# Two early blocks of the first expert in unsplit fp32 inside the last routing step, and every split of its weights behind the branch

## The chip, the cores and the metric

The kernel is one program on one core of a Trainium2 chip. The metric is its device time in microseconds (us), the median of the runs. TensorE (PE) multiplies; its weight loads are shown apart as PEld. VectorE (DVE), ScalarE (ACT) and GpSimd (POOL) work on elements, and SyncE (SP) issues most of the transfers. Each engine works through its own instructions in order and waits for the others by semaphores.

## The reference, cut to what matters

```python
def _moe_ref(x, w_gate, w_local, w1, w2):
    logits = np.einsum('bsd,de->bse', x, w_gate)
    local_gate = 1.0 / (1.0 + np.exp(-np.einsum('bsd,de->bse', x, w_local).squeeze(-1)))
    for b in range(B):
        prev_e = -1
        for s in range(S):
            fresh_e = int(np.argmax(logits[b, s]))
            e = fresh_e if s == 0 or local_gate[b, s] < 0.5 else prev_e
            prev_e = e
            ...
            h = np.maximum(x[b, s] @ w1[e], 0.0)
            out[b, s] = p[e] * (h @ w2[e])      # p: softmax of the logits
```

Ahead of it stands attention over the 32 largest scores (4 batches, 8 heads, 576 tokens, heads of 64). Its output, 4 x 576 tokens of 512 numbers, goes through this mixture of 8 experts with a hidden width of 1024, and the result through a Fourier mixing and a feed-forward layer. Everything is fp32.

## The kernel before

**Stages.** Attention runs first, in 16 pairs of heads with 9 tiles each; a batch is routed as soon as its last tile is done. The routing of the last batch, the *tail*, runs when attention has nothing left. Then all engines load the flag `slow_i` and branch (L1029, L1030; the branch to the exact path isn't taken). Behind the branch come the experts, in the order of their load (rank 0 to 7), then the mixing and the last layer.

**Split products.** The experts' products are made of three products of halves (`fp32r`): a high part (`whi`, `xh`, `hh`) times a high part, high times low, low times high. A weight unit of 128x2048 comes by one SP transfer of 1 MB into `raw` (two buffers), ACT writes `whi` (L214), and DVE or POOL writes `wlo = raw - whi` (L215), each in two halves of 1024 columns. A rank has four units, `wunits[0..3]` for rank 0: first and second layer of hidden blocks 0 to 3, then of blocks 4 to 7. For block f, `mm1` (L1151) makes 12 products, ACT `hh` (relu, L1155), DVE `hl` (L1156), and two steps later `mm2` (L1175) adds 6 products to the sum.

**Early rows.** Rank 0's expert is known after the third batch. Its first 256 rows (`EARLY`, in `xe`) are there before the tail; the other 256 rows come with the last scatter. Blocks f = 0 to 2 (`EF = 3`) of the early rows are done by `early_layers` inside the tail (L591, L604): a generator whose pieces `spend(us)` hands to PE between the routing's own products. Before that, `early_x` transposes the early rows on PE (L572) and splits them (L574 on ACT, L575 on DVE); units 0 and 1 are split between the last tiles of attention, halves of unit 2 on POOL in the tail, unit 3 behind the branch.

**The tail's chain.** DVE turns the last sums `st_x` into logits (`ri` L627, `ltt` L630, L657) and one-hot rows `dl` (L683). PE turns `dl` over (L692), DVE scans it to `er` and `po` (L700 to L708), PE turns those back (L715), DVE makes `oh` and the scatter's indices (L723 to L736), POOL scatters the tokens in five transfers (L751), and DVE and PE rank the experts and write `slow_i` (L776).

**Behind the branch.** SP loads the late rows; PE turns the four chunks of 128 rows (L1105), ACT and DVE split them (L1107, L1108). A hand-written plan then lists the blocks, (rank, f, early rows or not), `mm2` two steps behind `mm1`; splits, loads and a conversion of other weights (`fr`, `fa`, L1126 and L1050) are placed at certain steps of it. The products' results have two buffers, so a block's `mm1` waits until relu and `hl` of the block two before it are done.

```python
plan = [(0, f, True) for f in range(EF, 8)] + [(r, f, False) for r in range(E) for f in range(8)]
```

Of the kernel before, what the change touches and what calls it, by code (L numbers as in the profile page):

```python
# [104 lines left out]
def body(ctx: ExitStack, tc, q, k, v, w_gate, w_local, w1, w2, ch1, ch2, ts, tcd, tnd, tid, out, dbg=None):  # L105
# [76 lines left out]
    slot = [consts.tile([8, 1], F32, name=f"slot{b}") for b in range(B + 1)]  # L182
    DVE.tensor_scalar(slot[0], pcol[0:8], float(XC), None, op0=OP.mult)

    EARLY, EF = 256, 3
    late0 = consts.tile([8, 1], F32, name="late0")
    DVE.tensor_scalar(late0, pcol[0:8], float(XC), float(EARLY), op0=OP.mult, op1=OP.add)
    pv0 = consts.tile([128, 2, 1], F32, name="pv0")
    sid0 = consts.tile([128, 2, 1], I32, name="sid0")
    em0 = consts.tile([128, 2, 1], F32, name="em0")  # L190

    W = {}
    n_u = [0]

    def unit(key, src, dims, pool=None):


        if pool is None:
            pool = (wring, wring, wring, wring, wring2, wring2)[n_u[0] % 6]
            n_u[0] += 1  # L200
        raw, hl = [], []

        def load():
            raw.append(raws.tile([128, 2048], F32, name="raw", tag="raw"))
            SP.dma_start(raw[0].rearrange("p (c f) -> p c f", c=dims), src)

        def split(j, eng):
            if not hl:
                p = pool[0] if isinstance(pool, list) else pool
                hl.extend(p.tile([128, 2048], F32R, name=nm, tag="w") for nm in ("whi", "wlo"))  # L210
                W[key] = tuple(t.rearrange("p (c f) -> p c f", c=dims) for t in hl)
            hi, lo = hl
            cs = slice(1024 * j, 1024 * (j + 1))
            ACT.activation(hi[:, cs], raw[0][:, cs], AF.Copy)  # L214
            eng.tensor_tensor(lo[:, cs], raw[0][:, cs], hi[:, cs].bitcast(F32), op=OP.subtract)  # L215

        return load, split
# [53 lines left out]
    def attention(exact):  # L271
# [3 lines left out]
        with ExitStack() as ph:  # L275
# [10 lines left out]
            spb = acc[:, :, 0:288]  # L286
            if exact:
                for c in range(2):
                    PE.matmul(acc[:, c], W[0, 0, 1][0][:, 0, 0:128], W[0, 0, 1][0][:, 0, :], start=False, stop=True)
            rank_ps[0] = tkp  # L290
            ub = ps.tile([128, 512], F32, name="u", bufs=1)
            up = ub[:, 0:2 * VW].rearrange("p (s d) -> p s d", s=2)
# [271 lines left out]
            def early_x(c):  # L564

                if c == 0:
                    XE["hl"] = [ap.tile([128, 2, S], F32, name="kt", bufs=4).rearrange("p s c -> p (s c)")[:, 0:4 * EARLY]
                                .rearrange("p (d n) -> p d n", d=4) for _ in range(2)]
                x, (xh, xl) = xe, XE["hl"]
                p = next_wide()[:, 0:512]  # L570
                for d in range(4):
                    PE.transpose(p[:, 128 * d:128 * d + 128], x[:, c, 128 * d:128 * d + 128], ident)  # L572
                pr, n = p.rearrange("p (d n) -> p d n", d=4), slice(128 * c, 128 * c + 128)
                ACT.activation(xh[:, :, n].bitcast(F32R), pr, AF.Copy)  # L574
                DVE.tensor_tensor(xl[:, :, n].bitcast(F32R), pr, xh[:, :, n], op=OP.subtract)  # L575
                if c == 1:
                    DVE.tensor_copy(pv0, x[:, :, DM:DM + 1])
                    rows_of(sid0, x[:, :, DM + 2 * IW:DM + 2 * IW + 1], em0)

            def early_layers():  # L580

                xh, xl = (t.bitcast(F32R) for t in XE["hl"])
                hb = [[t.rearrange("p s c -> p (s c)")[:, EARLY * k:EARLY * k + EARLY] for k in range(3)] for t in qpb]
                pb = (wide[0][:, 0:EARLY], wide[1][:, 0:EARLY], wide[1][:, 512:512 + EARLY])
                for j in range(EF + 2):
                    if j < EF:
                        wh, wl = W[0, 0, 0]
                        p, fs = pb[j % 3], slice(j * 128, (j + 1) * 128)
                        for n, (a, x) in enumerate(((wh, xh), (wh, xl), (wl, xh))):
                            for d in range(4):  # L590
                                PE.matmul(p, a[:, d, fs], x[:, d], start=(n == 0 and d == 0), stop=(n == 2 and d == 3))  # L591
                            yield
                        hh, hl = hb[0][j % 3], hb[1][j % 3]
                        ACT.activation(hh.bitcast(F32R), p, AF.Relu)
                        DVE.scalar_tensor_tensor(hl.bitcast(F32R), p, 0.0, hh, op0=OP.max, op1=OP.subtract)
                    if j in (1, 2) and not exact:
                        wunits[2][1](j - 1, POOL)
                    if j >= 2:
                        f = j - 2
                        hh, hl = (t[f % 3].bitcast(F32R) for t in hb)  # L600
                        wh, wl = W[0, 0, 1]
                        for n, (a, w) in enumerate(((hh, wh), (hh, wl), (hl, wh))):
                            for c in range(2):
                                PE.matmul(acc[:, c], a[:, c * 128:c * 128 + 128], w[:, f, :],  # L604
                                          start=(f == 0 and n == 0), stop=False)
                            yield

            early = []

            def spend(us):  # L610
                while early and us > 0:
                    if next(early[0], 1):
                        early.pop()
                    us -= 0.47

            TK = {}

# [33 lines left out]
            def tokens(b):  # L651
# [57 lines left out]
                yield  # L709
                for o, r in ((8, er), (0, po)):  # L710
                    if b == B - 1:
                        spend(1.4 if o else 0.9)
                    for t in range(5):
                        m = 128 if t < 4 else LAST
                        PE.transpose(pt[0:m, t, o:o + 8], r[:, 128 * t:128 * t + m], ident[0:8, 0:8])  # L715
# [46 lines left out]
                    early_load(ex)  # L762
                if b == B - 1:
                    yield
                    if not exact:
                        check_end(chk.pop())
                    for _ in ranks(cnt[B], spend):
                        yield
                    spend(0.5)

                    ov = ap.tile([8, 1], F32, name="ov", bufs=1)
                    DVE.tensor_tensor(ov, cnt[B], capv, op=OP.is_gt)
                    p = tkp
                    PE.matmul(p[0:1, 0:1], ov, ones8[:, 0:1], start=True, stop=True)
                    yield
                    DVE.tensor_scalar(slow_i, p[0:1, 0:1], fail_f, 0.0, op0=OP.add, op1=OP.is_gt)  # L776
# [26 lines left out]
                chk.append(km)  # L803

            def check_end(km):
                p = tkp
                PE.transpose(p[0:1, 0:128], km[:, 0:1], ident)
                kr = ap.tile([1, 1], F32, name="kr", bufs=1)
                DVE.tensor_reduce(kr, p[0:1, 0:128], axis=AX.X, op=OP.min)
                DVE.tensor_scalar(fail_f, kr, 0.5, None, op0=OP.is_lt)  # L810
                DVE.tensor_copy(fail_i, fail_f)
# [86 lines left out]
            for n in range(n_tile + 1 + max(OFF.values())):  # L898
# [22 lines left out]
                    use_consts()  # L921
                if n == n_tile - 1 + OFF["z"]:
                    tok.append(check())
                e = n - n_tile - 3
                if e in (3, 4):
                    early_x(e - 3)
                if 2 <= e < 6:
                    wunits[(e - 2) // 2][1](e % 2, DVE)
                    if e % 2:
                        wunits[2 + (e - 2) // 2][0]()  # L930
            early.append(early_layers())
            for g in tok:
                for _ in g:
                    pass
# [131 lines left out]
    with ExitStack() as ph:  # L1066
# [135 lines left out]

        load_slots(0)
        p0 = prep(0)
        for o in p0[:2]:
            o()
        pops, us, spl = p0[2:], [], []
        for h in range(2):
            wunits[3][1](h, DVE)
        LAG = 2  # L1210
        plan = [(0, f, True) for f in range(EF, 8)] + [(r, f, False) for r in range(E) for f in range(8)]
        for j in range(len(plan) + LAG):
            if j < len(plan):
                r, f, early = plan[j]
# [1 line left out]
            if j >= LAG:  # L1216
                r2, f2, early2 = plan[j - LAG]
                mm2(r2, f2, early2)
                if f2 == 7 and not early2:
                    finish(r2)  # L1220
            if j < 8 - EF:
                if j in (3, 4):
                    pops.pop(0)()
                continue
            if j == 8 - EF:
                exs += [nc.values_load(exi[0:1, x:x + 1], engines=[mybir.EngineType.SP], min_val=0, max_val=E - 1)
                        for x in range(1, E)]
                load_slots(1)
                f64_load(0)
                f64_load(1)  # L1230
            if j == 10 - EF:
                POOL.dma_start(tst, ts)
            if j == 18 - EF:
                POOL.dma_start(tct, tcd)
                POOL.dma_start(tnt, tnd)
            if f in (0, 3, 4, 7) and spl:
                for h in range(2):
                    spl[0](h, DVE)
                spl.pop(0)
            if j >= len(plan):  # L1240
                continue

            if f in (0, 4):
                us = expert_units(r + 1, exs[r + 1], f // 4) if r + 1 < E else mix_units(f // 4)
                if r + 1 == E and f == 4:
                    m1 = list(us)
            if f in (0, 1, 4, 5):
                load, split = us.pop(0)
                if r + 1 < E or f < 2:
                    load()  # L1250
# [364 lines left out]
```

## Time and profile before

| what | us |
|---|---|
| runs | 1263.56, 1265.39, 1265.83 (median 1265.39) |
| the profiled execution | 1266.99 |
| its span, first to last instruction | 1264.8 |
| PE busy | 1194.6 (94% of the span) |
| DVE, ACT, POOL busy | 866.9, 676.3, 446.0 |

The span is 2.2 us shorter than its own execution's time. PE is busy nearly everywhere, except around the tail and the branch, which lie between about 473 and 511 us. A row of the timeline gives start, length, engine, line, operation, output and inputs, and in brackets how long the engine had been idle and what ended that.

### The profile page before, as it was taken

The numbers are of one execution on the slowest core, as the hardware profiler recorded it, in microseconds if no ns is written. First come the engines' busy times: TensorE is split into PE (matmuls) and PEld (weight loads), VectorE is DVE, ScalarE is ACT, GpSimd is POOL, SyncE is SP. The second block draws the span as 40 slices with busy tenths as digits, with TensorE's granted clock in tenths as the row PEclk, the third lists the DMA queues.
The fourth block names the chain that finished last, engine by engine and source line by source line (L and its number), as shares of the span: only waits on it lengthen the run. The fifth ranks groups of instructions, "written<-read, shape, count | busy, mean of one in ns | idle before, by whom it ended". The sixth has DMA issues, their size and how long they took to land. (4 is left out here: it accounts for less than half of the span.)

```text
span 1264.8 us, 25173 instructions
## 1 busy us (share of the span) xinstructions
PE 1194.6 (94%) x8691; PEld 1086.4 (86%) x8691; DVE 866.9 (69%) x3559; ACT 676.3 (53%) x1426; POOL 446.0 (35%) x553
## 2 busy tenths in 40 slices
PE   6999999999998995999999995979999999999997
PEld 5999889998998994898888885869999999999996
DVE  7999999999998985475666665847744444443222
ACT  6999999999997992354444542323322222221110
POOL 3767776786875683011111102713200000000122
PEclk9999999999998998999999995989999999999998
DMA  5757634443451413876666756632310010100111
GB/s 113 193 149 199 143 86 116 115 103 86 124 131 44 138 49 109 259 270 216 213 228 218 231 174 191 194 115 80 102 67 34 34 67 20 49 1 1 50 51 51
DMA packets 125653, 152.25 MB, mean 120 GB/s; under 512 B 68175, under 2 KB 70471, under 8 KB 125402
## 3 DMA queue, kind: packets, MB, share of 16 engines
q1 hardware_dynamic: 120442, 133.34, 36.8%
q0 software_dynamic: 5072, 17.19, 3.8%
q8 instruction: 71, 1.16, 0.4%
q14 instruction: 68, 0.56, 0.1%
HBM read 92.05 MB, written 32.79 MB: 99 GB/s over the span
## 5 line engine op out<-in xcount | busy, mean ns | idle before, releaser
L474 POOL TENSOR_TENSOR y<-ss,g 128x576 f32<-128x576 f32 x144 | 185.3, 1287 | 116.2 <-ACT g L469 58.3
L448 DVE MAX8 cd<-ss 128x8 f32<-128x72 f32 x1152 | 218.2, 220 | 10.0 <-ACT ss L442 9.5
L1529 ACT ACTIVATE fhh<-f 128x256 fp32r<-128x256 f32 x144 | 55.1, 383 | 278.9 <-PE f L1525 274.4
L1530 DVE SCALAR_TENSOR_TENSOR fhl<-f,fhh 128x256 fp32r<-128x256 f32 x144 | 60.9, 423 | 205.9 <-ACT fhh L1529 205.8
L545 PE MATMUL u<-in_v,et 128*128 128x74 f32 (+1 forms) x1600 | 185.5, 265 | 4.9 <-DVE dv L704 2.5
L545 PEld LDWEIGHTS u<-in_v,et 128*128 128x128 f32 (+1 forms) x1600 | 177.5, 181 | 10.0 <-ACT st_x L552 4.0
L528 PE MATMUL tp<-ident,z 128*128 128x128 f32 x720 | 142.6, 284 | 4.8 <-DVE lo L355 4.6
L529 PE MATMUL tp<-huge_id,bb 128*128 128x128 bf16 x720 | 131.7, 220 | 0.3 <-ACT bb L507 0.3
L435 PE MATMUL acc<-kt,qp 128*128 128x288 f32 x640 | 125.2, 323 | 6.3 <-ACT ss L442 4.0
L1550 POOL DMA_INDIRECT out_dram<-ut,orow x18 | 17.5, 971 | 319.4 <-DVE ut L1546 317.5
L469 ACT ACTIVATE g<-ss,mt 128x576 bf16<-128x576 f32 x144 | 118.0, 819 | 5.4 <-DVE mt L462 5.2
L528 PEld LDWEIGHTS tp<-ident,z 128*128 128x128 f32 x720 | 106.4, 148 | 15.6 <-POOL z L516 3.4
L507 ACT ACTIVATE bb<-ss,kth 128x576 bf16<-128x576 f32 x144 | 117.1, 813 | 0.0
L479 DVE MAX8 y<-y 128x8 f32<-128x576 f32 x144 | 107.0, 743 | 5.6 <-POOL y L474 5.6
L516 POOL TENSOR_SCALAR z<-ss,mt 128x576 f32<-128x576 f32 x144 | 107.8, 749 | 5.2 <-PE tp L529 5.2
L534 ACT ACTIVATE et<-tp 128x640 f32<-128x640 f32 x144 | 106.6, 740 | 2.4 <-PE tp L529 1.9
L442 ACT ACTIVATE ss<-acc 128x576 f32<-128x576 f32 x144 | 99.8, 693 | 11.6 <-PE acc L435 8.5
L941 POOL DMA_INDIRECT xm_d<-ysb,sid x23 | 24.6, 1068 | 228.8 <-ACT ysb L1187 225.1
L435 PEld LDWEIGHTS acc<-kt,qp 128*128 128x128 f32 x640 | 94.1, 197 | 9.7 <-ACT ss L442 5.0
L1525 PEld LDWEIGHTS f<-nxh,whi 128*128 128x128 f32 x576 | 87.8, 188 | 14.2 <-issue 1.2
L215 DVE TENSOR_TENSOR wlo<-raw,whi 128x1024 fp32r<-128x1024 f32 x70 | 85.5, 1260 | 14.8 <-ACT whi L214 14.4
L1541 PE MATMUL f<-whi,fhh 128*128 128x512 f32 x288 | 91.6, 399 | 0.7 <-ACT fhh L1529 0.7
(283 smaller groups left out, 2778.9 us busy)
## 6 DMA issues: line engine op xcount, KB each, us to landing
raw<-in_moe_w_dram SPq DMA_DIRECT2D x32, 1024.0 KB
kt<-hi SPq DMA_DIRECT2D x60, 144.0 KB
kt<-lo SPq DMA_DIRECT2D x60, 144.0 KB
xs_d<-xtok SPq DMA_DIRECT2D x8, 1056.0 KB
fr<-in_moe_w_ch_dram SPq DMA_DIRECT2D x16, 512.0 KB
raw<-in_moe_w_ch_dram SPq DMA_DIRECT2D x16, 512.0 KB
md<-md_d SPq DMA_DIRECT2D x9, 516.0 KB
in_k<-in_k_dram SPq DMA_DIRECT2D x32, 128.0 KB
```

The lines of the kernel that those rows point to most:

```text
L435: PE.matmul(p, QP[i][:, s, o:o + 128].bitcast(F32R), KT[i][j][:, s, c].bitcast(F32R), start=(s == heads[0] and j == 0), stop=(s == heads[- ...
L442: ACT.activation(t.rearrange("p (h c) -> p h c", h=2), spb, AF.Copy)
L448: return [lambda j=j: DVE.max(cd[:, 8 * j:8 * j + 8], SS[n][:, 72 * j:72 * j + 72]) for j in range(8)]
L469: ACT.activation(g, SS[n], AF.Sign, bias=MT[i][:, t, 1, 7:8], scale=-SCL, accum_out=DIF[n])
L474: POOL.tensor_tensor(y, SS[n], LT[n], op=OP.mult)
L479: DVE.max(y8, Y8[n])
L507: ACT.activation(t, SS[n], AF.Relu, bias=kth[:, n:n + 1], scale=-1.0)
L516: POOL.tensor_scalar(ZZ[n], SS[n], -1.0, MT[i][:, t, 0, 0:1], op0=OP.mult, op1=OP.add)
L528: PE.matmul(o, z[:, k], ident, start=True, stop=False, is_transpose=True)
L529: PE.matmul(o, bb[:, k], huge_id, start=False, stop=True)
L534: ACT.activation(et, TP.pop(n).rearrange("p (c n) -> p c n", c=5), AF.Exp, scale=-1.0)
L545: PE.matmul(p[0:m, s, 0:VW], et[:, kc, qs], vv[:, kc, VC[s]], start=(kc == 0), stop=(kc == 4))
```

## The change

`EF` falls from 3 to 2. `early_layers` now multiplies the unsplit `raw` weights by an unsplit copy of the early rows, in plain fp32: 8 products of 256 columns (L585), 4 of 512 (L592), and a relu on ACT for each block; a piece is one product, and `spend` counts 0.47 for the smaller and 0.93 for the larger. `early_x` makes one copy on ACT only, one step sooner. No unit is split and none of units 2 and 3 is loaded before the branch. Behind it, ACT and DVE split units 0 and 1 between the first two chunks of rows, SP loads units 2 and 3, and these are split at steps 1 and 2 of a new plan. The end of the check (`check_end`) goes behind two steps of the ranking. (Lines of the kernel after are 12 to 15 smaller than those of before.)

```diff
-    EARLY, EF = 256, 3
+    EARLY, EF = 256, 2
...
                 for d in range(4):
-                    PE.transpose(p[:, 128 * d:128 * d + 128], x[:, c, 128 * d:128 * d + 128], ident)
-                pr, n = p.rearrange("p (d n) -> p d n", d=4), slice(128 * c, 128 * c + 128)
-                ACT.activation(xh[:, :, n].bitcast(F32R), pr, AF.Copy)
-                DVE.tensor_tensor(xl[:, :, n].bitcast(F32R), pr, xh[:, :, n], op=OP.subtract)
...
+                    PE.transpose(p[:, 128 * d:128 * d + 128], xe[:, c, 128 * d:128 * d + 128], ident)
+                ACT.activation(XE["t"][:, :, 128 * c:128 * c + 128], p.rearrange("p (d n) -> p d n", d=4), AF.Copy)
...
-                    if j in (1, 2) and not exact:
-                        wunits[2][1](j - 1, POOL)
...
+                for f in range(EF):
+                    p = wide[1][:, 512 * f:512 * f + EARLY]
+                    for d in range(4):
+                        PE.matmul(p, w1_[:, d, 128 * f:128 * f + 128], XE["t"][:, d], start=(d == 0), stop=(d == 3))
+                        if d < 3:
+                            yield 0.47
+                    ACT.activation(hb[f], p, AF.Relu)
+                    yield 0.47
+                for f in range(EF):
+                    for c in range(2):
+                        PE.matmul(acc[:, c], hb[f][:, 128 * c:128 * c + 128], w2_[:, f, :], start=(f == 0), stop=False)
+                        yield 0.93
...
-                if 2 <= e < 6:
-                    wunits[(e - 2) // 2][1](e % 2, DVE)
-                    if e % 2:
-                        wunits[2 + (e - 2) // 2][0]()
+                e = n - n_tile - 1
+                if e in (4, 5):
+                    early_x(e - 4)
             early.append(early_layers())
+            spend(1.8)
...
         p0 = prep(0)
-        for o in p0[:2]:
-            o()
-        pops, us, spl = p0[2:], [], []
+        p0[0]()
         for h in range(2):
-            wunits[3][1](h, DVE)
+            wunits[0][1](h, DVE)
+        p0[1]()
+        for h in range(2):
+            wunits[1][1](h, DVE)
+        for load, _ in wunits[2:]:
+            load()
+        for f in range(EF, 4):
+            mm1(0, f, True)
+        for f in range(EF, 4):
+            mm2(0, f, True)
+            p0[f]()
+        pops, us, spl = [], [], []
         LAG = 2
-        plan = [(0, f, True) for f in range(EF, 8)] + [(r, f, False) for r in range(E) for f in range(8)]
+        plan = [(0, f, False) for f in range(4)] + [(0, f, e) for f in range(4, 8) for e in (True, False)]
+        plan += [(r, f, False) for r in range(1, E) for f in range(8)]
...
+            if j in (1, 2):
+                for h in range(2):
+                    wunits[j + 1][1](h, DVE)
```

DVE in the tail before, from the end of the check's work to the reduction that begins the routing's chain (`kt` are the split early rows):

```order
L215 TENSOR_TENSOR wlo<-raw,whi 128x1024
L627 TENSOR_SCALAR ri<-st_x 128x5 x2
L628 RECIPROCAL ri<-ri 128x5x2
L630 TENSOR_TENSOR ltt<-st_x,ri 128x5x9 x2
L575 TENSOR_TENSOR kt<-tp_148,kt 128x4x128
L577 COPY pv_128<-xe 128x2
L257 TENSOR_SCALAR em_130<-xe 128x2
L258 SCALAR_TENSOR_TENSOR sid_129<-xe,em_130 128x2
L215 TENSOR_TENSOR wlo<-raw,whi 128x1024 x2
L657 TENSOR_REDUCE dv<-ltt 128x45
```

The same piece after:

```order
L570 COPY pv_128<-xe 128x2
L258 TENSOR_SCALAR em_130<-xe 128x2
L259 SCALAR_TENSOR_TENSOR sid_129<-xe,em_130 128x2
L615 TENSOR_SCALAR ri<-st_x 128x5 x2
L616 RECIPROCAL ri<-ri 128x5x2
L618 TENSOR_TENSOR ltt<-st_x,ri 128x5x9 x2
L645 TENSOR_REDUCE dv<-ltt 128x45
```

The splits and the subtraction of the early rows are gone from between `ltt` and its reduction, and the three small operations stand ahead of `ri`.

PE in the tail before, from the products of `dl` to those of `po`:

```order
L692 MATMUL u<-ident,dl 8x64
L591 MATMUL tp_149<-kt,whi 128x256 x8
L591 MATMUL tp_149<-kt,wlo 128x256 x4
L715 MATMUL u<-ident,er 128x8 x4
L715 MATMUL u<-ident,er 64x8
L591 MATMUL tp_149<-kt,whi 128x256 x8
L715 MATMUL u<-ident,po 128x8 x4
```

The same piece after, with the early products ahead of `dl`:

```order
L585 MATMUL tp_149<-kt,raw 128x256 x7
L680 MATMUL tp_148<-ident,dl 8x128 x3
L680 MATMUL u<-ident,dl 8x128
L680 MATMUL u<-ident,dl 8x64
L585 MATMUL tp_149<-kt,raw 128x256
L592 MATMUL acc<-raw,kt 128x512
L703 MATMUL u<-ident,er 128x8 x4
L703 MATMUL u<-ident,er 64x8
L592 MATMUL acc<-raw,kt 128x512
L703 MATMUL u<-ident,po 128x8 x4
```

Between the routing's products stand single fp32 products now, and no product there reads a split weight.

ACT behind the branch before (`xh` are chunks of rows, the first `hh` belong to the early rows, the last two rows to block 0 of the late rows and to the conversion):

```order
L1107 ACTIVATE xh_17130<-tp 128x4x128 x2
L214 ACTIVATE whi<-raw 128x1024 x2
L1155 ACTIVATE hh<-m_17155 128x256
L1155 ACTIVATE hh<-m_17172 128x256
L1155 ACTIVATE hh<-m_17189 128x256
L1155 ACTIVATE hh<-m_17212 128x256
L1107 ACTIVATE xh_17130<-tp 128x4x128
L1155 ACTIVATE hh<-m_17242 128x256
L1107 ACTIVATE xh_17130<-tp 128x4x128
L1155 ACTIVATE hh<-m_17275 128x256
L1050 ACTIVATE fa<-fr 128x512
```

The same stretch after; `m_17110` is block 0 of the late rows, `m_17206` and `m_17232` are its blocks 1 and 2:

```order
L1092 ACTIVATE xh_17012<-tp 128x4x128
L215 ACTIVATE whi<-raw 128x1024 x2
L1092 ACTIVATE xh_17012<-tp 128x4x128
L215 ACTIVATE whi<-raw 128x1024 x2
L1140 ACTIVATE hh<-m_17047 128x256
L1140 ACTIVATE hh<-m_17064 128x256
L1092 ACTIVATE xh_17012<-tp 128x4x128 x2
L1140 ACTIVATE hh<-m_17110 128x256
L1035 ACTIVATE fa<-fr 128x512
L1140 ACTIVATE hh<-m_17206 128x256
L215 ACTIVATE whi<-raw 128x1024 x2
L1140 ACTIVATE hh<-m_17232 128x256
```

Two splits stand ahead of the second chunk's copy, five early blocks became two, and two more splits follow the conversion `fa` with a relu between them.

## Rows read from the trace of the kernel before

**Rows 1.** Timeline of the tail, ACT and DVE from the last sums to the routing's reduction:

```profile
478.08 0.27 ACT L554 ACTIVATE st_x<-u 64x148 f32<-64x148 f32 x1
478.22 1.23 DVE L215 TENSOR_TENSOR wlo<-raw,whi 128x1024 fp32r<-128x1024 f32 x1 [0.25 <-ACT whi L214]
...
479.36 0.24 DVE L627 TENSOR_SCALAR ri<-st_x 128x5 f32<-128x5 f32 x2
...
481.47 2.51 DVE L215 TENSOR_TENSOR wlo<-raw,whi 128x1024 fp32r<-128x1024 f32 x2
...
483.90 0.30 DVE L657 TENSOR_REDUCE dv<-ltt 128x45 f32<-128x135 f32 x1
```

**Rows 2.** Timeline of the tail, from the products of `dl` to those of `po`:

```profile
486.14 0.80 PE L692 MATMUL tp<-ident,dl 128*8 128x128 f32 x3 [2.35 <-DVE dl L683]
...
487.44 0.12 DVE L699 MEMSET u<- 128x80 f32 x1 [0.69 <-PE u L692]
...
489.13 1.40 DVE L708 TENSOR_TENSOR_SCAN po<-dv,slot,er 8x576 f32<-8x576 f32 x1
...
492.38 0.44 PE L715 MATMUL u<-ident,po 8*128 8x8 f32 x5
```

**Rows 3.** Windows: length, busy PE, PEld, DVE, ACT, POOL, TensorE clock, DMA share, GB/s:

```profile
480.00:490.00 10.00, 6.79 (x29) 5.70 (x29) 8.80 (x26) 1.35 (x3) 1.76 (x4) 0.51 0.67 211
...
507.00:511.00 4.00, 4.00 (x20) 4.00 (x21) 3.42 (x5) 2.07 (x3) 1.22 (x3) 0.52 1.17 333
511.00:546.00 35.00, 34.31 (x226) 30.59 (x225) 17.39 (x36) 13.36 (x26) 0.00 (x0) 1.00 0.81 267
```

**Rows 4.** One line's instructions (L1029, L1030), POOL's queue: ns, first and last start:

```profile
L1029 POOLq TENSOR_LOAD <-slow_i x1: 565/565/565, 499.9 to 499.9; - x1
...
L1030 POOLq EVENT_SEMAPHORE  x6: 17/30/43, 503.7 to 504.1; - x6
...
L1030 POOLq INC_SWDGE_SEM  x1: 591/591/591, 504.2 to 504.2; - x1
```

**Rows 5.** Timeline around and behind the branch, to the first second-layer products:

```profile
501.01 2.34 POOL L215 TENSOR_TENSOR wlo<-raw,whi 128x1024 fp32r<-128x1024 f32 x1
...
505.71 1.08 ACT L1107 ACTIVATE xh<-tp 128x512 fp32r<-128x512 f32 x2 [10.85 <-PE tp L1105]
...
506.68 2.00 ACT L214 ACTIVATE whi<-raw 128x1024 fp32r<-128x1024 f32 x2
...
506.90 1.19 PE L1151 MATMUL m<-xh,whi 128*128 128x256 f32 x4 [1.85 <-ACT xh L1107]
...
508.74 1.05 PE L1151 MATMUL m<-xh,wlo 128*128 128x256 f32 x4
...
509.59 1.05 PE L1151 MATMUL m<-xh,whi 128*128 128x256 f32 x4
...
512.98 0.62 PE L1175 MATMUL acc<-whi,hh 128*128 128x512 f32 x2
...
514.38 0.64 PE L1151 MATMUL m<-xh,whi 128*128 128x256 f32 x4
...
515.80 0.63 PE L1175 MATMUL acc<-whi,hh 128*128 128x512 f32 x2
```

**Rows 6.** Groups of PE instructions by shape: count, busy us, mean ns, idle before:

```profile
L545 PE MATMUL u<-in_v,et 128*128 128x74 f32 x1280 | 161.6, 274 | 4.1 <-DVE dv L704 2.5 <-ACT st_x L552 1.0 <-issue 0.4
```

**Rows 7.** Timeline from the last chunk's transposes to the conversion and the block behind it:

```profile
520.46 0.60 PE L1105 MATMUL tp<-ident,xsl 128*128 128x128 f32 x4
...
521.55 0.95 SPq L1126 DMA_DIRECT2D fr<-in_moe_w_ch_dram  x2
...
521.75 0.74 PE L1151 MATMUL m<-xh,whi 128*128 128x256 f32 x4 [0.69 <-ACT xh L1107]
...
528.36 0.68 ACT L1050 ACTIVATE fa<-fr 128x512 f32<-128x512 f32 x1 [4.26 <-DMA fr<-in_moe_w_ch_dram]
...
529.41 0.42 DVE L1156 SCALAR_TENSOR_TENSOR hl<-m,hh 128x256 fp32r<-128x256 f32 x1
```

More of the change, by code (lines that the diff above doesn't have):

```diff
@@ L190, in body @@
     em0 = consts.tile([128, 2, 1], F32, name="em0")
-    W = {}
+    W, RAW = {}, {}
     n_u = [0]
@@ L201, in unit @@
         raw, hl = [], []
+        RAW[key] = raw
         def load():
@@ L288, in attention @@
                 for c in range(2):
-                    PE.matmul(acc[:, c], W[0, 0, 1][0][:, 0, 0:128], W[0, 0, 1][0][:, 0, :], start=False, stop=True)
+                    PE.matmul(acc[:, c], ident, RAW[0, 0, 1][0][:, 0:512], start=False, stop=True)
             rank_ps[0] = tkp
@@ L566, in early_x @@
                 if c == 0:
-                    XE["hl"] = [ap.tile([128, 2, S], F32, name="kt", bufs=4).rearrange("p s c -> p (s c)")[:, 0:4 * EARLY]
-                                .rearrange("p (d n) -> p d n", d=4) for _ in range(2)]
-                x, (xh, xl) = xe, XE["hl"]
+                    XE["t"] = ap.tile([128, 2, S], F32, name="kt", bufs=4).rearrange("p s c -> p (s c)")[:, 0:4 * EARLY] \
+                        .rearrange("p (d n) -> p d n", d=4)
+                    DVE.tensor_copy(pv0, xe[:, :, DM:DM + 1])
@@ L570, in early_x @@
+                    rows_of(sid0, xe[:, :, DM + 2 * IW:DM + 2 * IW + 1], em0)
                 p = next_wide()[:, 0:512]
                 for d in range(4):
-                    PE.transpose(p[:, 128 * d:128 * d + 128], x[:, c, 128 * d:128 * d + 128], ident)
-                pr, n = p.rearrange("p (d n) -> p d n", d=4), slice(128 * c, 128 * c + 128)
-                ACT.activation(xh[:, :, n].bitcast(F32R), pr, AF.Copy)
-                DVE.tensor_tensor(xl[:, :, n].bitcast(F32R), pr, xh[:, :, n], op=OP.subtract)
@@ L576, in early_x @@
-                if c == 1:
-                    DVE.tensor_copy(pv0, x[:, :, DM:DM + 1])
-                    rows_of(sid0, x[:, :, DM + 2 * IW:DM + 2 * IW + 1], em0)
-            def early_layers():
[L582 to L595, printed above, removed]
-                    if j in (1, 2) and not exact:
-                        wunits[2][1](j - 1, POOL)
[L598 to L606, printed above, removed]
@@ new lines, in early_x @@
+                    PE.transpose(p[:, 128 * d:128 * d + 128], xe[:, c, 128 * d:128 * d + 128], ident)
+                ACT.activation(XE["t"][:, :, 128 * c:128 * c + 128], p.rearrange("p (d n) -> p d n", d=4), AF.Copy)
+            def early_layers():
+                w1_, w2_ = (RAW[0, 0, u][0].rearrange("p (c f) -> p c f", c=4) for u in range(2))
+                hb = ap.tile([128, 2, S], F32, name="kt", bufs=4).rearrange("p s c -> p (s c)")
+                hb = [hb[:, EARLY * f:EARLY * f + EARLY] for f in range(EF)]
+                for f in range(EF):
[10 more added lines that the diff above has]
+                        yield 0.93
@@ L611, in spend @@
                 while early and us > 0:
-                    if next(early[0], 1):
+                    t = next(early[0], 0)
+                    if not t:
                         early.pop()
-                    us -= 0.47
+                    us -= t
             TK = {}
@@ L711, in tokens @@
                     if b == B - 1:
-                        spend(1.4 if o else 0.9)
+                        spend(1.3 if o else 0.9)
                     for t in range(5):
@@ L764, in tokens @@
                     yield
-                    if not exact:
-                        check_end(chk.pop())
-                    for _ in ranks(cnt[B], spend):
+                    for k, _ in enumerate(ranks(cnt[B], spend)):
+                        if k == 2 and not exact:
+                            check_end(chk.pop())
                         yield
@@ L805, in check_end @@
             def check_end(km):
-                p = tkp
+                p = tkp[:, 256:384]
                 PE.transpose(p[0:1, 0:128], km[:, 0:1], ident)
@@ L923, in attention @@
                     tok.append(check())
-                e = n - n_tile - 3
-                if e in (3, 4):
-                    early_x(e - 3)
-                if 2 <= e < 6:
-                    wunits[(e - 2) // 2][1](e % 2, DVE)
-                    if e % 2:
-                        wunits[2 + (e - 2) // 2][0]()
+                e = n - n_tile - 1
+                if e in (4, 5):
+                    early_x(e - 4)
             early.append(early_layers())
+            spend(1.8)
             for g in tok:
@@ L1220, in body @@
                     finish(r2)
[L1221 to L1225, printed above, removed]
+            if j == 0:
                 exs += [nc.values_load(exi[0:1, x:x + 1], engines=[mybir.EngineType.SP], min_val=0, max_val=E - 1)
@@ L1230, in body @@
                 f64_load(1)
-            if j == 10 - EF:
+            if j in (1, 2):
+                for h in range(2):
+                    wunits[j + 1][1](h, DVE)
+            if early:
+                continue
+            if j == 2:
                 POOL.dma_start(tst, ts)
-            if j == 18 - EF:
+            if (r, f) == (1, 2):
                 POOL.dma_start(tct, tcd)
                 POOL.dma_start(tnt, tnd)
-            if f in (0, 3, 4, 7) and spl:
+            if f in ((4, 5, 7) if r == 0 else (0, 3, 4, 7)) and spl:
                 for h in range(2):
@@ L1241, in body @@
                 continue
-            if f in (0, 4):
+            if f in ((2, 5) if r == 0 else (0, 4)):
                 us = expert_units(r + 1, exs[r + 1], f // 4) if r + 1 < E else mix_units(f // 4)
@@ L1246, in body @@
                     m1 = list(us)
-            if f in (0, 1, 4, 5):
+            if f in ((2, 3, 5, 6) if r == 0 else (0, 1, 4, 5)):
                 load, split = us.pop(0)
```

## The prediction

> **What bounds the kernel now.** I read the windows first, then the timeline of the tail, the single instructions around the branch, and the timeline behind it. From 511 us on PE is busy 34.31 of 35.00 us at the full clock [rows 3]: behind the branch the order of PE's own work is the bound, and whatever is added there is paid in full. In the tail it is not. Between 480 and 490 us DVE is busy 8.80 of 10 us, PE 6.79, at a granted clock of 0.51 (the lower of its two levels, 1.2 GHz). DVE's chain sets the end there, and three things stand in it: a split ahead of `ri`, two more ahead of the reduction [rows 1], and PE's early products, which make `po` wait [rows 2]. POOL's way over the branch is the last to open the part behind it [rows 4, 5].
>
> **What the tail gains.** The last sums end at 478.35, yet `ri` starts at 479.36, because a half split of 1.23 sits on DVE [rows 1]. That split goes, and one ACT half split (half of the 2.00 pair [rows 5]) no longer stands beside the last sums, where the copy of the early rows now stands: I take 1.2 for both. From `ri` to the reduction there are 4.54 us (479.36 to 483.90), of which two splits take 2.51 and the early rows' work most of the rest; the five small operations that stay, at 0.24 for two, are about 0.8. So 3.7 more, and `dl` is ready 4.9 us earlier, at 481.2 instead of 486.14 [rows 2].
>
> PE must be free by then. Seven products of 256 columns now stand ahead of `dl`. No row shows a plain fp32 product of that width. From below, a transposing fp32 product of 128 columns takes about 0.12 (four rows in 0.60 less the last one's tail [rows 7]), so 0.23 for 256. From above, the fp32 products of 74 columns come as two records each of about 0.12 (161.6 us for 1280, mean 274 ns with overlap [rows 6]), so 0.24 for 74 and 0.83 for 256; that row is mostly weight load, so it is loose. The code itself charges 0.47, four times the split kernel's product (1.42 us for 12 [rows 5]), and I take that: 3.3 us from about 478.0, when both copies are there, to 481.3. That is just when `dl` is ready. It costs nothing, or 2.5 us at the upper bound. The Trainium skill (FP8 and Floating Point Precision, section TensorE Precision Notes) says that true FP32 makes four passes through the array; by that the seven products would be 3.3 us, which no run here shows yet.
>
> `dl`'s products and what follows them, 1.30 us at the lower clock (486.14 to 487.44 [rows 2]), can be at most 0.45 shorter if PE has stayed busy; I take 0.3. The scan of `po` ends at 490.53, but PE turns it only at 492.38 [rows 2]: 1.85 late, behind eight early products. After, between `dl` and `po` PE has 0.47 + 0.93 + 0.93 of early work and the five small products of `er`, under the 3.1 us that DVE takes (487.44 to 490.53). So 1.7 of it goes. The gain is 4.9 + 0.3 + 1.7 = **6.9 us** (6.4 to 7.4) at `oh`, the scatters and `slow_i`; behind `oh` the chain keeps its operations and a like sum of early work.
>
> Whether the restart follows is POOL's matter. It loads the flag at 499.9, behind its fourth scatter, begins again at 503.7, ends its last step of 591 ns at 504.8, and ACT starts 0.9 later [rows 4, 5]. Its split ends at 503.35, just under 503.7, so taking that split away gains at most 0.35 by itself, and nothing while the branch takes 3.8 us from the load. The scatters move with `oh`, so the first `xh` starts at 505.71 - 6.9 = 498.8.
>
> **What is paid behind the branch.** (a) Before, the first product follows the first `xh` by 1.19. Now ACT makes `xh` (half of 1.08), two `whi` (2.00) and `xh` again before the first product can run [rows 5]: 3.1. So 1.9 of the gain is gone, and the first product starts 5.0 earlier. (b) One early block more: 1.42 for its first layer, 1.40 for its second [rows 5], **+2.8**. (c) The second four products need the second `xl`. On DVE it stands behind two `wlo` (2.46 [rows 1]) that can begin 1.5 after the start, and takes 0.65: ready at 4.6, wanted at 3.1 + 0.85 = 3.95, **+0.7**. (d) Clock: 0.52 in 507 to 511 [rows 3]; four products take 0.85 there (508.74 to 509.59) and 0.47 later [rows 5], so before pays 1.8 for some five groups. PE is idle over the branch as before and now stalls in its first block too, so it pays this again and I add **+0.8** (0 to 1.6).
>
> (e) The conversion `fa` stands on ACT right behind relu of late block 0 and ahead of relu of block 1, in both kernels, and waits for `fr`. Before, `fr` is issued at 521.55, `fa` starts at 528.36, and block 1's `hl` ends at 529.83, 9.4 us after the last chunk's transposes (520.46 [rows 7]). PE doesn't notice, since it has early blocks to finish: 1.29 to the first product, three first layers of 1.42, one second layer of 1.40, which makes 7.0, and two more second layers of early blocks (2.8), 9.8 in all. After, those two have moved away; PE comes to block 3's first layer, which needs block 1's buffer, after 7.0. With the landing of before, **+2.4**. The landing may move either way. What is queued behind it: relu 1, two `whi`, relu 2 and all of PE. SP now issues units 2 and 3 (2 MB) ahead of `fr`, beside POOL's tables; in 507 to 511, with the tables alone, the row shows 333 GB/s at a DMA share of 1.17 [rows 3], that is full. At that rate 2 MB is 6 us, most of which is over before `fr` is issued some 10 us after the restart. I take **+2.6** (0.8 to 4). The Trainium skill (DMA: Bandwidth & Descriptors, section Issuing engines are not separate DMA queues) has transfers of all issuers interleave on the same 16 engines. This speaks against the change: by that, whatever is left of the 2 MB delays `fr`, and (e) goes to its upper end.
>
> (f) Units 2 and 3 are split right behind: relu 1, `whi` (2.00), and on DVE two `wlo` (2.46) ahead of block 2's `hl` (0.42). From block 1's `hl` this is about 3.7 us, against 2.8 of PE's work; the next pair adds a little: **+1.2** (0 to 2).
>
> Sum: -5.0 + 2.8 + 0.7 + 0.8 + 2.6 + 1.2 = **+3.1 us**. Against the profiled execution (1266.99, span 1264.8 and 2.2 around it) this is 1270.1; that execution lies 1.6 above the median of the runs, so against the median 1265.39 it is **1268.5**. The bounds of all terms together give -2.1 (the gain 7.4, (d) to (f) at nothing) and +6.7. From rank 1 on both plans are alike, so the difference stays.
>
> **The rivals.** *No change that can be measured* (under 0.2%, 2.5 us, which is about what a measurement of this kernel tells from none): `fr` lands early. Rank 1's unit loads, which before follow it on SP after some 1 us, are now at later steps; `fr` and the rows of rank 1 are 1.8 MB, 5.5 us at 333 GB/s, against the 6.8 of before. Then (e) is about 0.8 and (f) half: +3.1 - 1.8 - 0.6 = +0.7, **1266.1**. Against it speak the 2 MB ahead on the same queue.
>
> *Faster*: one mechanism, the clock. PE has work through the whole tail now, and the restart comes sooner; if its clock is still up when it starts behind the branch, (d) is not +0.8 but -1.8, and with (e) and (f) hidden as well by a landing under 4.5 us, the sum is -5.0 + 2.8 + 0.7 - 1.8 = -3.3, **1262.1**. It decides at a clock near 1.0 at the first block. Against it: before, PE worked up to the branch too and still restarted at 0.52 [rows 3].
>
> *Much slower*: the fp32 products cost 0.83 and hold the routing. `dl` then waits 2.5, `po` about 1, the ranking 1.5: 5 us on top of +3.1, **1273.5**. The clock at the lower level in the tail would do the same.
>
> *The change doesn't do what it says* in one point: the free POOL buys nothing, as its split ended ahead of its restart. The sum counts it so.
>
> **How the numbers follow.** The forecast has 0.52, with a range of its own of 1267 to 1271; 0.10 of that ends within 2.5 us. No change has 0.27, faster 0.13, much slower 0.08. So faster 0.13, same 0.37, slower 0.50. The range from 1262.5 to 1272.0 leaves out half of the faster case, the much slower one, and a rest of the forecast, 0.2 together.
>
> **What would show it.** `dl` products near 481, `po` products right behind its scan, first `xh` near 499, first product of the experts near 502, and from there each loss in its place: the second four products waiting for `xl`, `fa` waiting for `fr` and block 3's products behind it, the clock by windows. The first 384-column product of rank 1 should start some 3 us later than before. The prediction is wrong if the tail gains much under or over 6.9, if `fr` lands before ACT wants it, or if rank 1's units, now loaded and split a step later, come late for rank 1's first block, which the sum doesn't hold.

## The result: slower by 0.6%, and where it shows

| kernel | median us | lowest to highest | against before |
|---|---|---|---|
| before, 7 runs | 1266.32 | 1263.56 to 1266.52 | |
| after, 7 runs | 1272.99 | 1270.10 to 1275.08 | 1.0058 (1.0045 to 1.0071) |

The change costs 6.7 us between the medians; forecast were 3.1 and a range up to 1272.0. The direction was right, the size was not.

The profiled execution of after spans 1271.2 us, that of before 1264.8. Attention itself ends 1.2 us earlier in after's. Before's execution spent all of 402 to 412 us at a clock of 0.51, after's had 0.83 there, and so had a variant of before that was profiled later. So from here on times are counted from the last tile's exponential on ACT (`et`), at 472.70 in before and 471.48 in after.

| from the last `et`, us | before | after | difference |
|---|---|---|---|
| start of the write of `slow_i` | 25.29 | 17.81 | -7.5 |
| first `xh` behind the branch | 33.01 | 25.73 | -7.3 |
| first product of rank 0 | 34.20 | 28.80 | -5.4 |
| end of rank 0 (first output row scaled) | 79.44 | 88.74 | +9.3 |
| end of the span | 792.09 | 799.66 | +7.6 |

The tail does what it was changed to do, and more is lost inside rank 0 than was won. The timeline of after's tail, columns as in [rows 1] and [rows 2] (lines ahead of the change are one larger than before's, so L555 is before's L554):

```profile
476.37 0.28 ACT L555 ACTIVATE st_x<-u 64x148 f32<-64x148 f32 x1
...
476.53 1.99 PE L585 MATMUL tp<-kt,raw 128*128 128x256 f32 x8 [0.69 <-ACT kt L575]
476.68 0.24 DVE L615 TENSOR_SCALAR ri<-st_x 128x5 f32<-128x5 f32 x2 [4.93 <-ACT st_x L555]
...
477.56 0.32 DVE L645 TENSOR_REDUCE dv<-ltt 128x45 f32<-128x135 f32 x1
...
480.39 0.49 PE L680 MATMUL tp<-ident,dl 128*8 128x128 f32 x3
...
481.24 0.12 DVE L687 MEMSET u<- 128x80 f32 x1 [0.35 <-PE u L680]
...
482.92 1.41 DVE L696 TENSOR_TENSOR_SCAN po<-dv,slot,er 8x576 f32<-8x576 f32 x1
...
484.39 0.45 PE L703 MATMUL u<-ident,po 8*128 8x8 f32 x5
```

`ri` starts at the end of the last sums, the reduction 0.88 behind it (4.54 in [rows 1]), and PE turns `po` at 484.39, where the scan ends at 484.33; in [rows 2] it came 1.85 late. Eight records of L585 are four products in 1.99 us, so a plain fp32 product of 256 columns takes two records and at most 0.50 together. The clock stayed up in this tail, where before had 0.51 from 480 to 490 [rows 3]; columns as there:

```profile
476.00:487.00 11.00, 9.74 (x42) 5.45 (x42) 7.93 (x35) 1.54 (x5) 2.08 (x5) 1.00 0.00 1
```

Behind the branch the same view of after shows the loss:

```profile
497.21 0.60 ACT L1092 ACTIVATE xh<-tp 128x512 fp32r<-128x512 f32 x1 [15.02 <-PE tp L1090]
...
497.70 1.99 ACT L215 ACTIVATE whi<-raw 128x1024 fp32r<-128x1024 f32 x2
...
500.28 1.20 PE L1136 MATMUL m<-xh,whi 128*128 128x256 f32 x4 [3.15 <-ACT xh L1092]
...
502.40 1.22 PE L1136 MATMUL m<-xl,whi 128*128 128x256 f32 x4 [0.93 <-DVE xl L1093]
...
511.74 0.96 SPq L1111 DMA_DIRECT2D fr<-in_moe_w_ch_dram  x2
...
522.55 0.66 ACT L1035 ACTIVATE fa<-fr 128x512 f32<-128x512 f32 x1 [8.23 <-DMA fr<-in_moe_w_ch_dram]
523.12 0.37 ACT L1140 ACTIVATE hh<-m 128x256 fp32r<-128x256 f32 x1
...
523.59 0.42 DVE L1141 SCALAR_TENSOR_TENSOR hl<-m,hh 128x256 fp32r<-128x256 f32 x1
...
524.06 1.22 PE L1136 MATMUL m<-xh,whi 128*128 128x256 f32 x4 [5.95 <-DVE hl L1141]
```

This is the chain to read backwards. PE stands still for 5.95 us ahead of late block 3, because its buffer is block 1's, whose `hl` (523.59) is late, because relu (523.12) is late, because `fa` stands ahead of it on ACT and waits 8.23 us for `fr`. `fr` is issued at 511.74, and `fa` starts 10.8 us later; in [rows 7] it was 6.8, and PE didn't notice. The same place holds PE once more, by 0.92, at the conversion's second chunk, where `fa` waits 4.39 us for the store of the first chunk. Both are in this line of after's waits from 495 to 556 us (us in total, times, longest):

```profile
PE m L1136 <- DVE hl L1141: 6.9, 2, 5.9
```

After's windows, columns as in [rows 3], show what the wait does to the clock:

```profile
491.00:508.00 17.00, 8.73 (x35) 7.90 (x36) 6.67 (x8) 5.63 (x8) 3.41 (x7) 0.50 0.72 182
508.00:517.70 9.70, 9.01 (x59) 7.78 (x59) 2.11 (x6) 1.58 (x3) 0.00 (x0) 0.99 1.06 368
517.70:524.00 6.30, 0.41 (x2) 0.00 (x0) 0.75 (x2) 1.45 (x3) 0.00 (x0) 0.83 0.59 232
524.00:528.60 4.60, 4.54 (x17) 4.15 (x18) 4.11 (x7) 3.81 (x6) 0.00 (x0) 0.50 0.15 7
```

The clock had come up at 508, fell in the wait, and the next 4.6 us of full work ran at 0.50, the lower level: five groups that take 0.47 at the upper level took 0.85, about 2 us more. And the transfer engines were full, 368 GB/s at a share of 1.06, up to the wait and some 3 us into it.

### The profile page after: what moved, and what is told of

Same layout as the page of the kernel before. It is cut to its first block, busy times and chain, and to the rows that moved or that the text cites. A ratio compares the mean times of both kernels' runs of the same rounds, so it can differ in the third digit from the quotient of the medians.

```text
span 1271.2 us, 25143 instructions
## 1 busy us (share of the span) xinstructions
PE 1193.8 (94%) x8679; PEld 1084.2 (85%) x8679; DVE 866.9 (68%) x3557; ACT 674.7 (53%) x1426; POOL 441.4 (35%) x551
## 5 line engine op out<-in xcount | busy, mean ns | idle before, releaser
L216 DVE TENSOR_TENSOR wlo<-raw,whi 128x1024 fp32r<-128x1024 f32 x72 | 87.7, 1257 | 13.5 <-ACT whi L215 13.3
```

## The experiments

**The conversion later.** The kernel after, with rank 0's first chunk four blocks later and the next two caught up in rank 1:

```diff
-            f64_step(2 * r + f // 4, f % 4)
+            if r == 0:
+                if f >= 4:
+                    f64_step(0, f - 4)
+            elif r == 1 and f < 4:
+                for h in range(2):
+                    f64_step(1 + f // 2, 2 * (f % 2) + h)
+            else:
+                f64_step(2 * r + f // 4, f % 4)
```

> The kernel after, with rank 0's first conversion (fa on ACT) four late blocks further on and the next one caught up in rank 1, so that no relu of rank 0's first blocks stands behind fr. Theory A (the wait for fr is what the change lost): PE's wait of 5.95 us ahead of late block 3, the half-clock stretch that follows it (about 2 us) and the later wait of 0.92 go, 1272.99 falls by 7.5 to 9 to about 1264 to 1265.5. Rival B (the splits of units 2 and 3 hold PE at the same place anyway): the gain is at most 3, 1270 or more.

Measured: 1263.86 us, 0.9975 of before (0.9957 to 0.9993). 9.1 us less than after (the runs of before beside it have 1266.33), with every product, split and transfer still there. PE's waits in it, from 492 to 558 us, and its windows:

```profile
PE tp L1090 <- SPq L1015: 6.0, 1, 6.0
PE m L1136 <- ACT xh L1092: 3.8, 2, 3.1
PE m L1136 <- DVE xl L1093: 0.7, 1, 0.7
```

```profile
498.00:504.00 6.00, 4.64 (x20) 4.38 (x21) 5.19 (x6) 2.85 (x5) 0.11 (x1) 0.51 1.09 296
504.00:540.00 36.00, 35.31 (x234) 31.64 (x233) 20.09 (x36) 15.53 (x27) 0.00 (x0) 1.00 0.83 287
```

The wait for `hl` is gone, and from 504 on PE is busy 35.31 of 36.00 us at the full clock. Rank 0 ends 77.98 us after the last `et`, 10.8 sooner than in after. Theory A holds. Rival B falls: the splits of units 2 and 3 stand where they stood, and PE doesn't wait for them.

**`fr` ahead of units 2 and 3.** The kernel after with the two loads moved up on SP's queue:

```diff
         load_slots(0)
+        f64_load(0)
+        f64_load(1)
         p0 = prep(0)
...
                 load_slots(1)
-                f64_load(0)
-                f64_load(1)
```

> The kernel after, with the two loads of fr issued right behind the late rows' loads, ahead of units 2 and 3. Theory A: fr is there before ACT comes to the conversion, so 6 to 8 us go, less what the 1 MB delays units 2 and 3: 1265 to 1268. Rival B: units 2 and 3 land 2.5 us later and hold PE instead, 1270 or more.

Measured: 1267.89 us, 1.0015 of before (1.0001 to 1.0029). 5.1 us of after's loss go, and the time is the upper end of the 1265 to 1268 that theory A named. What was moved up has moved something else back; one line of PE's waits of this kernel from 492 to 560 us, and one of its timeline:

```profile
PE tp L1096 <- DMA xsl<-xs_d: 4.5, 1, 4.5
```

```profile
517.24 2.00 ACT L215 ACTIVATE whi<-raw 128x1024 fp32r<-128x1024 f32 x2 [4.17 <-DMA raw<-in_moe_w_dram]
```

PE waits for the rows of rank 1, now late behind unit 3, until 522.05. ACT waits 4.17 us for unit 2, and relu of block 2 stands behind that split, so its `hl` ends only at 522.09, and PE's next block needs its buffer. What rival B named is there too, then, but it costs less than the move gains.

**The tables later.** The kernel after with POOL's three table loads (2.8 MB) behind rank 0's store:

```diff
-            if j == 2:
-                POOL.dma_start(tst, ts)
-            if (r, f) == (1, 2):
-                POOL.dma_start(tct, tcd)
-                POOL.dma_start(tnt, tnd)
...
                 store(r - 1)
+                if r == 1:
+                    POOL.dma_start(tst, ts)
+                    POOL.dma_start(tct, tcd)
+                    POOL.dma_start(tnt, tnd)
```

> The kernel after, with POOL's three table loads (2.8 MB) moved behind rank 0's store. Theory C (fr lands late because 2.8 MB of tables and 2 MB of units share the transfer engines with it): fr lands 5 to 6 us after its issue instead of 10.8, PE's wait falls from 5.95 to 1 or 2, and the time to 1266 to 1268. Rival D (the landing is late by the order on SP's queue alone): fr lands no more than 2 us sooner, 1271 or more.

Measured: 1267.7 us, 1.001 of before (0.9999 to 1.0022), 5.3 less than after. Its timeline, and the line of PE's waits for `hl`:

```profile
510.23 0.96 SPq L1111 DMA_DIRECT2D fr<-in_moe_w_ch_dram  x2
...
515.63 0.67 ACT L1035 ACTIVATE fa<-fr 128x512 f32<-128x512 f32 x1 [2.82 <-DMA fr<-in_moe_w_ch_dram]
```

```profile
PE m L1136 <- DVE hl L1141: 3.6, 3, 2.2
```

`fa` starts 5.4 us after the issue instead of 10.8, though the order on SP's queue has not changed. So half of the landing time comes from POOL's transfers on the same engines: theory C, against the order on SP's queue alone. They had held up units 2 and 3 more than `fr` itself: without them the units are over when `fr` is issued (from 508 to 510.2 the engines move nothing). Of PE's waits for `hl`, 0.55 is left at late block 3 and 0.81 behind it; the 2.2 are at the second chunk.

**The control.** The kernel before with the first experiment's edit.

> The kernel before with the same move of the conversion as in the first run. Theory A: before hides its wait for fr behind two early blocks, so nothing changes: 1265.5 to 1267. Rival: before paid for it too, and gains 2 us or more.

Measured: 1267.26 us, 1.001 of before (0.9995 to 1.0026): no change. Before has the same wait of ACT for `fr` (4.26 us [rows 7]) and pays nothing for it that the medians show, as its early blocks cover it. In the one profiled execution of this kernel rank 0 ends 82.31 us after the last `et`, 2.9 later than in before's; 1.8 of that is there at the first `xh` (34.80), ahead of any conversion, so two executions of the same tail differ by that much.

**Four variants on what is left.** With the wait away, I tried the other terms. The first gives the conversion the same lag through all ranks, with the last chunks caught up in rank 7.

> The first run's kernel with the conversion's chunks simply four blocks later through all ranks and caught up in rank 7, so that no chunk's store stands behind a load that waits. Theory A says that rank 1's idle 1.3 us of the first run (ACT held 7.4 us by the store of the chunk before) comes back: 1262 to 1263. Rival: ACT's wait there was hidden, nothing changes, 1263.9.

Measured: 1264.6 us, 0.9988 of before (0.997 to 1.0006). No gain over 1263.86 that could be told from the scatter (1262.99 to 1267.96). In the trace rank 0 to 7 takes 207.6 us instead of 208.9 (from the first scaled output row to the last), so the 1.3 us are there in one execution; the medians don't show them.

The second, on the first experiment's kernel like the third, has three early blocks in fp32:

```diff
-    EARLY, EF = 256, 2
+    EARLY, EF = 256, 3
...
-                    p = wide[1][:, 512 * f:512 * f + EARLY]
+                    p = wide[1][:, 512 * (f % 2):512 * (f % 2) + EARLY]
...
-            p0[f]()
+        p0[2]()
+        p0[3]()
```

> The first run's kernel with three early blocks in plain fp32 (EF = 3): four products of 256 columns and two of 512 more in the tail, one block less behind the branch. Theory (term b of the sum, +2.8 for the block that the change moved behind the branch, and PE is idle in the tail from 487 to 495): 2 to 2.8 less than 1263.9, so 1261 to 1262. Rival: the added products hold the routing, 1263.5 or more.

Measured: 1264.79 us, 0.9975 of before (0.9958 to 0.9991): a miss, the 2 to 2.8 us don't appear. The execution that was profiled was the slowest of its runs (1269.18), so its trace says little on the median; in it PE waits 4.2 us for a split and 2.1 for the late rows.

The third makes `whi` of units 0 and 1 on ACT and `wlo` of unit 0 on POOL in the tail, where both are idle (a new last argument of a split: 1 makes `whi` alone, 2 `wlo` alone):

```diff
                 ACT.activation(pr, dl, AF.Exp)
+                if b == B - 1 and not exact:
+                    for h in range(2):
+                        wunits[0][1](h, POOL)
...
                         spend(1.3 if o else 0.9)
+                        if not o and not exact:
+                            for h in range(2):
+                                wunits[1][1](h, DVE, 1)
...
         p0[0]()
-        for h in range(2):
-            wunits[0][1](h, DVE)
         p0[1]()
         for h in range(2):
-            wunits[1][1](h, DVE)
+            wunits[1][1](h, DVE, 2)
```

> The first run's kernel with whi of units 0 and 1 made by ACT and wlo of unit 0 by POOL inside the tail, where both are idle, and both chunks of rows first behind the branch. Theory (terms a and c, 1.9 and 0.9): the first product follows the first xh by 1.2 instead of 3.1 and the next four don't wait, 2 to 2.8 less than 1263.9: 1261 to 1262. Rival: POOL's split or ACT's work holds the routing's chain or the scatters, 1263.5 or more.

Measured: 1265.63 us, 0.9998 of before (0.9978 to 1.0018): a miss too. The first product does follow the first `xh` by 1.2 us instead of 3.1, and `slow_i` is no later (17.81), so the edit works where it stands. But rank 0 ends at 78.31, against 77.98 without it. In its trace PE now waits 0.9 us for the late rows and 0.9 for those of rank 1; what else takes the gain isn't shown.

All three together:

> The three moves together (conversion four blocks later throughout, three early blocks, splits in the tail). If the terms add up: 1263.9 - 1.3 - 2.4 - 2.4, about 1258, 1257 to 1260. If they take the same idle time from each other: no better than the best of the three, 1261 or more.

Measured: 1266.79 us, 1.0 of before (0.9982 to 1.0018). In its trace PE, now early, waits for the late rows; one line of its waits, and its windows:

```profile
PE tp L1098 <- DMA xsl<-xs_d: 3.8, 1, 3.8
```

```profile
503.00:507.00 4.00, 0.18 (x2) 0.21 (x3) 0.91 (x3) 0.60 (x1) 0.00 (x0) 1.00 1.03 259
507.00:511.00 4.00, 3.31 (x17) 3.08 (x16) 0.87 (x3) 0.60 (x1) 0.00 (x0) 0.58 1.07 392
```

PE does 0.18 us of work in 4, the transfer engines are full (1.03), and the next 4 us run at 0.58. In this execution the work that was saved behind the branch has uncovered a transfer, and the clock adds to it. It is the fastest of the ten (1260.84), so its length says nothing on the median; but rank 0 ends in it 77.66 us after the last `et`, hardly sooner than in the first experiment (77.98).

**All three, and the tables later.** The same kernel with the third experiment's edit:

> The three moves together, and POOL's tables (2.8 MB) behind rank 0's store. In the profile of the three moves PE waits 3.8 us for the last late rows at 503 to 507 and the clock falls again after it. Theory C (behind the branch transfers are the bound once the work is less): the late rows and units land earlier, that wait and its half-clock stretch (about 2 us) go, 1266.8 falls to 1260 to 1262. Rival: the median stood still because the added work in the tail costs elsewhere; no change, 1265 or more.

Measured: 1262.01 us, 0.9951 of before (0.9931 to 0.9972), 5.3 us less than the runs of before beside it and faster than both kernels of this case. Its waits of PE from 492 to 560 us are

```profile
PE tp L1098 <- PEq L1023: 4.0, 1, 4.0
PE m L1144 <- ACT xh L1100: 1.9, 2, 1.2
PE acc L1168 <- ACT hh L1148: 0.5, 1, 0.5
PE m L1144 <- DVE xl L1101: 0.4, 1, 0.4
```

The wait for a transfer is gone, and rank 0 ends 73.52 us after the last `et`, 5.9 before the kernel before.

The counterpart, the tables' move with two early blocks and splits behind the branch:

> The kernel with the conversion four blocks later throughout, and the tables behind rank 0's store. Theory C: with two early blocks still behind the branch nothing waits for a transfer there (PE's waits are 3.1, 0.7 and 0.7 us, all for ACT and DVE), so the tables' place changes nothing: 1263.5 to 1265. Rival: the shared transfers cost there too, 1262 or less.

Measured: 1265.42 us, 0.998 of before (0.9962 to 0.9997), against 1264.6 with the tables in their old place: a little above the time named, and no change between the two beyond their scatter. With PE's waits for ACT and DVE, as here, moving the tables bought nothing that could be measured.

## Why the prediction was wrong, step by step

**The tail: right.** Forecast was a gain of 6.9 us (6.4 to 7.4), `dl` products near 481, `po` right behind its scan. Counted from the last `et`, 7.5 were gained at `slow_i` and 7.3 at the first `xh` (9.1 there against the control's execution, which has before's tail). The restart moved with the flag and the scatters, and POOL's free time bought at most 0.3, as said: POOL begins again 3.5 us after its load of the flag, 3.8 in [rows 4].

```profile
L1014 POOLq TENSOR_LOAD <-slow_i x1: 574/574/574, 491.7 to 491.7; - x1
...
L1015 POOLq EVENT_SEMAPHORE  x6: 17/30/43, 495.2 to 495.6; - x6
```

**The fp32 products: right.** 0.47 was taken between bounds of 0.23 and 0.83, and four products took 1.99. So the rival in which they hold the routing fell. This rests on a clock of 1.00 in the tail, for which the sum gave no reason (before's row had 0.51), so here it was lucky. The Trainium skill (FP8 and Floating Point Precision, section TensorE Precision Notes) gives true FP32 four passes; the trace agrees, with at most 0.50 a product against the 0.12 of a split kernel's product [rows 5].

**(a) to (d): right in size.** The first product follows `xh` by 3.07 (3.1 said), at 5.4 sooner than before (5.0 said). The second four products wait 0.93 for `xl` (0.7 said). The extra block (2.8) is plain work. The clock: before it was low for 3.9 us from the first product, in after for 7.8, to 508.1. Six groups of first-layer products at 0.85 instead of 0.47 and two of the second layer lose 2.9 us to it in after; before lost 1.9, so +1.0 (0.8 said).

**(e), the wait for `fr`: this is the step that failed.** The sum took the landing of before and put 0.2 on top (+2.6, bounds 0.8 to 4). The mechanism was the right one, with its place: `fa` ahead of relu 1 ahead of PE's block 3. Its size was off: PE waited 5.95 us. Counted from the last chunk's transposes (510.68), PE came to block 3 after 7.4 us (7.0 said), and block 1's `hl` ended after 13.3 (9.4 said): 2.0 of the wait are the lost cover, 3.9 the later landing. With the clock, two things went wrong. First, I reckoned that most of the units' 2 MB would be over when `fr` is issued. But a unit's load waits until the unit before it in its buffer is split, so they went out only 1.5 and 4.4 us after the first product, beside the tables: 4.8 MB in all. After's transfers from 498 to 510 us and from 510 to 523, by queue (q0 is POOL's, q1 SP's; packets, MB, share of 16 engines):

```profile
q0 software_dynamic: 241, 2.22, 74.3%
q1 hardware_dynamic: 371, 0.71, 25.1%
...
q1 hardware_dynamic: 1658, 3.78, 77.0%
q0 software_dynamic: 175, 0.66, 13.7%
```

The tables went first. Of SP's 3.78 MB, `fr` and the rows of rank 1 are 1.86, so at 510 some 1.9 of the units' 2.1 MB were still to come, and 1.7 when `fr` was issued. The issue-to-start time was 10.8, and 5.4 once the tables were away. The rule of the Trainium skill that I cited there (DMA: Bandwidth & Descriptors, section Issuing engines are not separate DMA queues) pointed the right way, and the trace agrees that all issuers share the engines, by the 5.4 without POOL's transfers; I gave it the upper bound of 4, which was not enough. Second, I counted the clock in (d) and not in (e): behind this wait of 6 us the clock was at its lower level (0.50), which cost about 2 us. With the 0.92 that the same conversion cost at its second chunk, (e) is 5.95 + 2 + 0.9 = 8.9 instead of 2.6. The first experiment took it away and gained 9.1. Of the signs of being wrong that the prediction named none came; `fr` landing later than before was not among them.

**(f), the splits of units 2 and 3: +1.2 said, nothing seen in after.** There PE was held anyway; in the first experiment, with nothing else in the way, PE doesn't wait for them either. With the tables later, PE does wait 0.81 us for block 2's `hl`, which on DVE stands behind these splits and two steps of the conversion.

Put together by what was measured: -5.4 + 2.8 + 0.9 + 1.0 + 8.9 + 0 = +8.2, against +9.3 at the end of rank 0; the rest of 1.1 stays open, and is less than the 2.9 by which before's and the control's executions differ at that place. Of the 9.3, 1.7 don't reach the end of the span: before's profiled execution spends 88.4 us between the last rank's output and the last layer's first relu, after's 86.8. The other kernels', with the same code there, lie between 85.8 and 88.6, so this looks like scatter; no run was made to settle it.

**The rivals.** The faster case rested on a clock still up at the restart; it was 0.50 from 491 to 508. The case of no change rested on `fr` landing sooner than before; it landed 4.0 later. The much slower case came near in size (1273.5 against 1272.99), by another cause than the one it named.

**The range.** The bounds of all terms, with (d), (e) and (f) all at their ends, add up to +6.6 (the prediction has +6.7), about the 6.7 that the medians show. From the three runs' median, 1265.39, that is 1272.0, where the range stopped; from the 1266.32 of seven runs it is 1272.9, and the time was 1272.99. So 0.9 of the distance is the time of before, and the rest is that (e) alone went far over its bound.

## What to carry to other kernels

A wait that is free today is free because of the work that runs beside it. Whoever moves that work has to ask for every wait in the stretch how long its cover was: here two early blocks (2.8 us) had covered a transfer, and the change also put 2 MB of units ahead of it. Size such a wait from the bytes that are under way on all queues at the time, not from how long the same transfer took before, and add what the lower clock costs behind it. And an element of little urgency (a conversion needed hundreds of microseconds later) doesn't belong in an in-order queue ahead of what the busy engine waits for; moving it gave 9 us, and the catching up in rank 1 cost 1.3 at most, by one trace.

## What the runs showed of the hardware

A wait of PE of 5.95 us cost about 8: the granted clock was 0.99 ahead of it, and 0.50 for the 4.6 us of full work behind it. The three moves together showed the same with a wait of 3.8 us (0.58 in the 4 us behind). So with transfers at their limit, less work on PE brought no gain that could be measured (1.0 of before, 0.9982 to 1.0018), and 0.9951 once 2.8 MB were moved out of the way.

Transfers of two queues did not share the engines evenly. In after a unit was issued on SP's queue at 501.77 and another at 504.64, with POOL's tables under way; from 504 to 510 the tables moved 1.21 MB in 169 packets and SP's queue 0.18 MB in 93. Why is not shown.

A plain fp32 product of 256 columns shows as two records with a weight load each, at most 0.50 us together (four in 1.99), about four times the 0.12 of one product of the split kernel.
